# Attention units of a transformer block: the order of ScalarE's first exponentials, two groups of sums, the distance tables first, two more zero products

## The chip, the cores and the metric

The kernel runs on one core of one Trainium2 chip. The metric is the device time of one execution in microseconds (us). A core has five engines with instruction queues of their own: TensorE (PE), VectorE (DVE), ScalarE (ACT), GpSimd (POOL) and SyncE (SP), which here issues most DMA transfers. They meet through semaphores.

## The reference

Attention with a distance bias over q, k and v of 2 batches x 8 heads x 768 positions x 64, and behind it two feed-forward layers on the 1536 x 512 result:

```python
scores = scale * np.matmul(q, k.transpose(0, 1, 3, 2))
rel = pos[:, None] - pos[None, :]
is_global = pos[None, :] < int(n_global)                 # 8
is_local = (rel >= 0) & (rel < int(n_local))             # 96
keep = is_global | is_local
dist = np.where(is_global & ~is_local, float(n_local), np.abs(rel).astype(np.float32))
bias = -slopes[:, None, None] * dist[None, :, :]
scores = np.where(keep, scores + bias[None], -1000000000.0)
scores = scores - np.max(scores, axis=-1, keepdims=True)
a = np.exp(scores)
a = a / (np.sum(a, axis=-1, keepdims=True) + 1e-09)
x = np.matmul(a, v)                                      # then as 1536 x 512
...
h = x @ w_in;  g = h * (1.0 / (1.0 + np.exp(-h)));         x = g @ w_out      # 512 -> 2048 -> 512
h = x @ w_in;  g = h * np.clip(h + 3.0, 0.0, 6.0) / 6.0;   x = g @ w_out
```

## The kernel before

Attention is cut into 16 **units**: a batch, a half of the sequence (384 positions) and a pair of heads. A unit has three query tiles of 128 rows (HB = 3); because a row keeps only the 96 positions behind it and 8 global ones, each tile needs 128 columns of keys (the first of a first half) or 256. Units 0 to 3 are the first half of batch 0. The main loop runs in steps n = 3u + t, tile t of unit u, and does at each step a part of several units:

- `loads`, `loads_v`: SP issues the DMAs for keys rk, kp, queries rq and values rv, vp of units ahead (L230 to L251).
- `stage_a` (t = 0 keys, t = 1 queries of unit u + 1): PE transposes them into the bank psA (L329 to L338), ACT copies the keys to kt (L350) and scales the queries into qt (L331), DVE copies the global keys into kt (L351, and L353 in a second half).
- `scores` (t = 0): six products of PE into the banks psS (L369).
- `exponentials`: DVE adds the bias and takes the row minimum (L379: z, mn), then ACT takes the exponential with the sum beside it (L383: z, sm). Two heads make a pair of each.
- `normalise`, one unit later: DVE adds 1e-9 to the sums and takes the reciprocal (L388, L389), POOL multiplies z with it (L393).
- `turn` (t = 2 of the next unit): PE transposes z into psT (L403); the copies pt go to DVE (L408, tiles 0 and 2) and ACT (L406, tile 1).
- `values` (two units later): PE multiplies with v into psO (L421); ACT writes the rounded copy xh (L424), DVE the rest xl (L425).

The bias tables come first: `positions` (POOL, DVE), then `patterns` (DVE, L277 to L294), which needs the two words n_global and n_local (nwords, L741) and leaves distB and distA; `biases` (POOL, L314) scales them for each pair of heads into nbB and nbA. `beyond` (L300 to L305) writes a flag that tells whether n_global and n_local lie outside what the tiling covers; it is read long after. Three products of zeros (L739, into psW) open the work of PE.

Beside attention the first feed-forward weights are decoded into a high and a low part: ACT L103, L107, L145, DVE L986 to L1003, POOL L126, L134, L148 (wih and wil are the parts of the weight, raw, da, dc, de the steps to them). From step 17 on a feed-forward piece (`h_piece`, psH, L482, or `y_piece`, psY, L655) is put in at every second step, and behind the last unit only these are left.

PE, ACT and POOL execute in the order in which this code is written. DVE and SP are ordered by a scheduler during attention, from the written order and the dependencies. Buffers of z, pt and the psum banks go round, so a tile waits for the one that had its place before.

Of the kernel before, what the change touches and what calls it, by code (L numbers as in the profile page):

```python
# [18 lines left out]
P = 128  # L19
# [9 lines left out]
def attention_ffn_kernel(ctx, tc, q, k, v, n_global, n_local, w_in1, w_out1, w_in2, w_out2, out):  # L29
# [345 lines left out]
    def exponentials(u, t):  # L375
        p, w = units[u][2], width(u, t)
        nb, z, mn, sm = nbs[p][w == W], zt[u], mnt[u], smt[u]
        for h in range(2):
            nc.vector.tensor_tensor_reduce(  # L379
                out=z[:, t, h, :w], in0=scored[u][h, t][:, :w], in1=nb[:, h, :], scale=1.0, scalar=3e38,  # L380
                op0=ALU.add, op1=ALU.min, accum_out=mn[:, t, h:h + 1])
        for h in range(2):
            nc.scalar.activation(out=z[:, t, h, :w], in_=z[:, t, h, :w], func=AF.Exp, bias=mn[:, t, h:h + 1], scale=-1.0,  # L383
                                 accum_out=sm[:, t, h:h + 1])

    def normalise(u):
        z, sm = zt[u], smt[u].rearrange("p t h -> p (t h)")
        nc.vector.tensor_scalar(out=sm, in0=sm, scalar1=1e-9, scalar2=None, op0=ALU.add)  # L388
        nc.vector.reciprocal(sm, sm)  # L389
        for t in range(HB):  # L390
            w = width(u, t)
            for h in range(2):
                nc.gpsimd.tensor_scalar(out=z[:, t, h, :w], in0=z[:, t, h, :w], scalar1=smt[u][:, t, h:h + 1], scalar2=1.0,  # L393
                                        op0=ALU.mult, op1=ALU.mult)
# [16 lines left out]
    def values(u):  # L411
# [12 lines left out]
        nc.scalar.copy(hi, ps[:, :TB])  # L424
        return lambda: nc.vector.tensor_tensor(out=lo, in0=ps[:, :TB], in1=hi.bitcast(F32), op=ALU.subtract)  # L425

    NS = HB * len(units)
    queue, late, rests, now = {}, {}, {}, [0]

# [3 lines left out]
    def attention_loop(n):  # L433
        u, t = divmod(n, HB)
        for f in queue.pop(n, []):
            f()
        if t == 0 and u < len(units):
            scores(u)
        if t == 0 and 0 <= u - 2 < len(units):
            at(n + 1, values(u - 2))  # L440
            if u < len(units):
                loads_v(u)
        if u < len(units):
            exponentials(u, t)
            if t == HB - 1 and u + 1 < NP:
                biases(u + 1)
        if n == 0:
            beyond()
        if t == 0 and 0 <= u - 1 < len(units):
            normalise(u - 1)  # L450
        for f in rests.pop(n, []):
            f()
        if t < 2 and u + 1 < len(units):
            stage_a(u + 1, t)
            if t and u + 3 < len(units):
                loads(u + 3)
# [277 lines left out]
    with tc.manual_schedule(engines=None):  # L734
        nc.vector.memset(three, 3.0)
        warm = fpool.tile([P, 512], F32, name="warm", tag="a")
        nc.vector.memset(warm, 0.0)
        for _ in range(3):
            nc.tensor.matmul(bank("f", "psW"), warm[:, :P], warm, start=True, stop=True)  # L739
        for i, ap in enumerate((n_global, n_local)):  # L740
            nc.sync.dma_start(nwords[:, i, :], ap.bitcast(I32).partition_broadcast(P))  # L741
        loads(0)
        make_identity(nc, ident)
        positions()
        loads(1)
        load_weights()
        loads_v(0)
        load_weights()
        loads(2)
        loads_v(1)  # L750
        load_weights()
        stage_a(0, 0)
        stage_a(0, 1)
        patterns()
        biases(0)
    todo = {when(i): f for i, f in enumerate(stream)}

    def loop(n):
# [277 lines left out]
```

## Time and profile before

| | |
|---|---|
| median of 3 runs | 636.79 us (635.8 to 637.16) |
| profiled execution | 634.86 us, its span 632.8 us |
| granted TensorE clock, mean | 0.992 of full speed |
| PE busy | 606.6 us (96%), 3124 products |
| DVE, ACT, POOL busy | 464.5 (73%), 412.9 (65%), 160.4 us (25%) |
| DMA | 97.29 MB, mean 154 GB/s |

The profiled execution has a start and an end of 2.06 us outside its span. A row of a timeline gives the start from the span's beginning, the duration, the engine, the line, the output and the inputs; in the brackets stands how long the engine had been idle just before and what released it. A row of the windows gives a stretch, its length and the busy time of PE, the weight loads of PE, DVE, ACT and POOL in it (with the number of instructions), then the clock that PE was granted, the busy share of the DMA engines, and GB/s. A clock of 1.00 is 2.4 GHz and 0.5 is 1.2 GHz; a stretch in which both occur has a mean between.

### The profile page before, as it was taken

The numbers are of one execution on the slowest core, as the hardware profiler recorded it, in microseconds if no ns is written. First come the engines' busy times: TensorE is split into PE (matmuls) and PEld (weight loads), VectorE is DVE, ScalarE is ACT, GpSimd is POOL, SyncE is SP. The second block draws the span as 40 slices with busy tenths as digits, with TensorE's granted clock in tenths as the row PEclk, the third lists the DMA queues.
The fourth block names the chain that finished last, engine by engine and source line by source line (L and its number), as shares of the span: only waits on it lengthen the run. The fifth ranks groups of instructions, "written<-read, shape, count | busy, mean of one in ns | idle before, by whom it ended". The sixth has DMA issues, their size and how long they took to land.

```text
span 632.8 us, 9365 instructions
## 1 busy us (share of the span) xinstructions
PE 606.6 (96%) x3124; PEld 496.4 (78%) x3124; DVE 464.5 (73%) x1012; ACT 412.9 (65%) x863; POOL 160.4 (25%) x233
## 2 busy tenths in 40 slices
PE   6877999999999999999999999999999999999996
PEld 3656778898888788888888877887788888888885
DVE  5776777734588786767674779987979696969453
ACT  4785878755566676666666676765766666666760
POOL 2764867770111111111111110011111111111100
PEclk9998999999999999999999999999999999999998
DMA  7665556367767858686867791196577768776544
GB/s 173 154 157 124 128 142 147 87 195 141 157 129 158 186 135 183 151 186 151 186 152 154 161 207 67 67 266 151 136 174 163 176 162 177 160 183 151 100 109 162
DMA packets 81622, 97.29 MB, mean 154 GB/s; under 512 B 55456, under 2 KB 55456, under 8 KB 81312
## 3 DMA queue, kind: packets, MB, share of 16 engines
q0 software_dynamic: 12576, 45.09, 38.1%
q1 hardware_dynamic: 68992, 51.53, 27.2%
q8 instruction: 27, 0.44, 0.3%
q14 instruction: 27, 0.22, 0.1%
HBM read 46.27 MB, written 3.15 MB: 78 GB/s over the span
## 4 chain that ended last, share of the span: by engine, by line
PE 58%; issue 23%; POOL 6%; DVE 5%; ACT 5%; DMA 2%; POOLq 0%; DVEq 0%; SPq 0%; ACTq 0%
PE psY L655 25%; PE psH L482 15%; POOL y L684 4%; PE psP_b L563 3%; PE psO L421 3%; PE psT L403 2%; PE psP_c L563 2%; PE psP_a L563 2%; PE psS_S L369 2%; ACT z L383 2%; DMA y<-st 1%; POOL z L393 1%; PE psW L739 1%; PE psS_o L369 1%; DVE z L379 1%
## 5 line engine op out<-in xcount | busy, mean ns | idle before, releaser
L684 POOL DMA_DIRECT2D y<-st x78 | 66.9, 857 | 364.3 <-ACT st L680 359.1
L680 ACT COPY st<-psY 128x512 f32<-128x512 f32 x156 | 91.5, 587 | 52.0 <-PE psY L655 47.9
L482 PE MATMUL psH<-xh,wih 128*128 128x512 f32 (+1 forms) x216 | 83.3, 386 | 2.1 <-DVE g L513 1.5
L482 PE MATMUL psH<-xh,wil 128*128 128x512 f32 (+1 forms) x216 | 82.7, 383 | 2.3 <-POOL wil L148 2.3
L482 PE MATMUL psH<-xl,wih 128*128 128x512 f32 (+1 forms) x216 | 82.7, 383 | 0.0
L655 PE MATMUL psY<-gh,woh 128*128 128x512 f32 (+1 forms) x160 | 61.4, 384 | 0.0
L655 PE MATMUL psY<-gh,wol 128*128 128x512 f32 (+1 forms) x160 | 60.6, 379 | 0.0
L655 PE MATMUL psY<-gl,woh 128*128 128x512 f32 (+1 forms) x160 | 60.5, 378 | 0.0
L655 PE MATMUL psY<-woh,gl 128*128 128x512 f32 x144 | 56.1, 390 | 0.1
L655 PE MATMUL psY<-woh,gh 128*128 128x512 f32 x144 | 56.1, 390 | 0.1
L655 PE MATMUL psY<-wol,gh 128*128 128x512 f32 x144 | 56.0, 389 | 0.0
L393 POOL TENSOR_SCALAR z<-z,sm 128x256 f32<-128x256 f32 (+1 forms) x96 | 45.9, 501 | 26.8 <-DVE sm L389 20.3
L383 ACT ACTIVATE z<-z,mn 128x256 f32<-128x256 f32 (+1 forms) x96 | 46.4, 489 | 3.8 <-DVE mn L379 3.7
L482 PEld LDWEIGHTS psH<-xh,wih 128*128 128x128 f32 x216 | 40.6, 188 | 10.6 <-DVE g L513 1.9
L482 PEld LDWEIGHTS psH<-xh,wil 128*128 128x128 f32 x216 | 40.7, 188 | 9.8 <-POOL wil L148 2.7
L103 ACT ACTIVATE da<-raw 128x512 f32<-128x512 f32 x64 | 43.0, 672 | 6.7 <-DMA raw<-in_moe_w_in_dram 5.3
L482 PEld LDWEIGHTS psH<-xl,wih 128*128 128x128 f32 x216 | 40.7, 188 | 7.5 <-DVE xl L592 0.4
L998 DVE SCALAR_TENSOR_TENSOR da<-raw,da 128x512 int32<-128x512 int32 x64 | 44.2, 690 | 1.1
L986 DVE TENSOR_SCALAR da<-da 128x512 f32<-128x512 f32 x64 | 29.5, 461 | 15.9 <-ACT da L103 15.6
L580 DVE TENSOR_TENSOR u<-psP_c,u 128x512 f32<-128x512 f32 x22 | 15.1, 686 | 34.6 <-ACT u L574 34.6
L504 ACT ACTIVATE a<-psH 128x512 f32<-128x512 f32 (+1 forms) x24 | 14.2, 590 | 40.2 <-PE psH L482 40.2
L523 DVE SCALAR_TENSOR_TENSOR gl<-a,gh 128x512 fp32r<-128x512 f32 (+1 forms) x34 | 23.1, 681 | 22.4 <-ACT gh L517 22.1
(187 smaller groups left out, 1496.9 us busy)
## 6 DMA issues: line engine op xcount, KB each, us to landing
y<-st POOLq DMA_DIRECT2D x78, 512.0 KB, 5.0
raw<-in_moe_w_in_dram SPq DMA_DIRECT2D x32, 512.0 KB, 4.0
raw<-in_moe_w_out_dram SPq DMA_DIRECT2D x32, 512.0 KB, 3.6
rk<-in_k_dram SPq DMA_DIRECT2D x32, 96.0 KB, 3.4
rq<-in_q_dram SPq DMA_DIRECT2D x32, 96.0 KB, 2.5
rv<-in_v_dram SPq DMA_DIRECT2D x32, 96.0 KB, 2.4
out_dram<-y SPq DMA_DIRECT2D x12, 256.0 KB, 2.6
xf<-xh SPq DMA_DIRECT2D x2, 1024.0 KB, 5.2
```

Of the source, the lines that this page charges most:

```text
L103: nc.scalar.activation(out=t["a"], in_=raws[n][:, :, 1].bitcast(F32), func=AF.Abs)
L369: nc.tensor.matmul(place[h, t], qt[hs, t * P:(t + 1) * P], kt[hs, o:o + W], start=True, stop=True)
L383: nc.scalar.activation(out=z[:, t, h, :w], in_=z[:, t, h, :w], func=AF.Exp, bias=mn[:, t, h:h + 1], scale=-1.0, accum_out=sm[:, t, h:h + 1])
L393: nc.gpsimd.tensor_scalar(out=z[:, t, h, :w], in0=z[:, t, h, :w], scalar1=smt[u][:, t, h:h + 1], scalar2=1.0, op0=ALU.mult, op1=ALU.mult)
L482: nc.tensor.matmul(ps, a[:, kt, js], x[:, kt, n0:n1], start=n == 0, stop=n == 3 * KT - 1)
L523: nc.vector.scalar_tensor_tensor(out=gl[:, j, :], in0=t["a"], scalar=2.0, in1=gh[:, j, :].bitcast(F32), op0=ALU.mult, op1=ALU.subtract)
L563: nc.tensor.matmul(ps, a[:, 2 * k + q, f * P:(f + 1) * P], x, start=p in (1, 5) and n == 0, stop=n == 5, skip_group_check=True)
L655: nc.tensor.matmul(ps[:, :rhs.shape[1]], lhs, rhs, start=n == 0, stop=n == 3 * FC - 1)
L680: nc.scalar.copy(st[:, m % 2, :], part)
L684: late.setdefault(n, []).append(lambda: nc.gpsimd.dma_start(y, st, accum_op=ALU.add))
L986: nc.vector.tensor_scalar(out=a, in0=a, scalar1=as_float(897 << 20), scalar2=as_float((1151 << 20) - 1), op0=ALU.max, op1=ALU.min)
L998: nc.vector.scalar_tensor_tensor(out=ai, in0=w1, scalar=-0x40000000, in1=ai, op0=ALU.bitwise_and, op1=ALU.bitwise_or)
```

## The change

Five things are moved or added, all in the attention part.

1. `exponentials(u, 0)` is now written ahead of `values(u - 2)`, so that ACT takes the first pair of exponentials of a unit ahead of the copy xh.
2. `normalise` is split: the sums of tiles 0 and 1 are taken at step t = 1 of the unit itself, those of tile 2 at t = 2. Before, all six came at t = 0 of the next unit.
3. `patterns` and `biases(0)` are written ahead of unit 0's `stage_a`; `biases` of the next unit move from t = 2 to t = 0.
4. `beyond` moves from step 0 to step 30.
5. Two more products of zeros stand at step 2, ahead of unit 1's scores on PE.

```diff
--- before.py
+++ after.py
@@ -383,11 +383,11 @@
             nc.scalar.activation(out=z[:, t, h, :w], in_=z[:, t, h, :w], func=AF.Exp, bias=mn[:, t, h:h + 1], scale=-1.0,
                                  accum_out=sm[:, t, h:h + 1])
 
-    def normalise(u):
-        z, sm = zt[u], smt[u].rearrange("p t h -> p (t h)")
+    def normalise(u, t0, t1):
+        z, sm = zt[u], smt[u][:, t0:t1].rearrange("p t h -> p (t h)")
         nc.vector.tensor_scalar(out=sm, in0=sm, scalar1=1e-9, scalar2=None, op0=ALU.add)
         nc.vector.reciprocal(sm, sm)
-        for t in range(HB):
+        for t in range(t0, t1):
             w = width(u, t)
             for h in range(2):
                 nc.gpsimd.tensor_scalar(out=z[:, t, h, :w], in0=z[:, t, h, :w], scalar1=smt[u][:, t, h:h + 1], scalar2=1.0,
@@ -424,6 +424,11 @@
         nc.scalar.copy(hi, ps[:, :TB])
         return lambda: nc.vector.tensor_tensor(out=lo, in0=ps[:, :TB], in1=hi.bitcast(F32), op=ALU.subtract)
 
+    def warm_up(n):
+
+        for _ in range(n):
+            nc.tensor.matmul(bank("f", "psW"), warm[:, :P], warm, start=True, stop=True)
+
     NS = HB * len(units)
     queue, late, rests, now = {}, {}, {}, [0]
 
@@ -434,22 +439,24 @@
         u, t = divmod(n, HB)
         for f in queue.pop(n, []):
             f()
-        if t == 0 and u < len(units):
-            scores(u)
+        if u < len(units):
+            if t == 0:
+                scores(u)
+                if u + 1 < NP:
+                    biases(u + 1)
+            exponentials(u, t)
+            if t:
+                normalise(u, *((0, 2), (2, 3))[t - 1])
         if t == 0 and 0 <= u - 2 < len(units):
             at(n + 1, values(u - 2))
             if u < len(units):
                 loads_v(u)
-        if u < len(units):
-            exponentials(u, t)
-            if t == HB - 1 and u + 1 < NP:
-                biases(u + 1)
-        if n == 0:
+        if n == 30:
             beyond()
-        if t == 0 and 0 <= u - 1 < len(units):
-            normalise(u - 1)
         for f in rests.pop(n, []):
             f()
+        if n == 2:
+            warm_up(2)
         if t < 2 and u + 1 < len(units):
             stage_a(u + 1, t)
             if t and u + 3 < len(units):
@@ -735,8 +742,7 @@
         nc.vector.memset(three, 3.0)
         warm = fpool.tile([P, 512], F32, name="warm", tag="a")
         nc.vector.memset(warm, 0.0)
-        for _ in range(3):
-            nc.tensor.matmul(bank("f", "psW"), warm[:, :P], warm, start=True, stop=True)
+        warm_up(3)
         for i, ap in enumerate((n_global, n_local)):
             nc.sync.dma_start(nwords[:, i, :], ap.bitcast(I32).partition_broadcast(P))
         loads(0)
@@ -749,10 +755,10 @@
         loads(2)
         loads_v(1)
         load_weights()
+        patterns()
+        biases(0)
         stage_a(0, 0)
         stage_a(0, 1)
-        patterns()
-        biases(0)
     todo = {when(i): f for i, f in enumerate(stream)}
 
     def loop(n):
```

What this makes of the engines' queues is shown at three places. In the names the first digit is the unit and the last number a buffer: kt3 are the keys of unit 3.

DVE at the start of the program, two pieces of the difference (+ is after, - before; distA and pat2 are the tables, small and nval the words, psA0_0 the transposed keys, psS0 the scores of unit 0):

```order
 L271 CAST pat2_87<-pat1_86 128x128
 L272 TENSOR_SCALAR pat2_87<-distA_83 128x256
-L351 COPY kt0_157<-psA0_0_159 128x2x32
 L277 SCALAR_TENSOR_TENSOR small_85<-nwords_82 128x2
 L278 SCALAR_TENSOR_TENSOR nval_59<-small_85,nwords_82 128x2
```

```order
 L294 TENSOR_SCALAR distA_83<-distA_83,nval_59 128x32
 L284 TENSOR_SCALAR pat2_87<-pat2_87 128x256
-L379 ISA z0_203,mn0_204<-psS0_S0_193,nbB0_184 128x128
+L285 TENSOR_TENSOR distA_83<-distA_83,pat2_87 128x256
+L351 COPY kt0_176<-psA0_0_178 128x2x32
+L379 ISA z0_203,mn0_204<-psS0_S0_193,nbB0_170 128x128
 L379 ISA mn0_204 128x1
```

The copy of unit 0's keys has moved from ahead of the tables to behind the last of them, and the first reduction stands behind both.

ACT between units 1 and 2, before and after:

```order
L406 COPY pt0_1_335<-psT0_1_330 128x512
L424 CAST xh_80<-psO0_358 128x384
L383 ACTIVATE z2_355,sm2_357<-z2_355,mn2_356 128x128 x2
L350 COPY kt3_390<-psA3_0_392 128x3x128
L103 ACTIVATE da1_400<-raw1_137 128x512
```

```order
L406 COPY pt0_1_345<-psT0_1_340 128x512
L383 ACTIVATE z2_365,sm2_367<-z2_365,mn2_366 128x128 x2
L424 CAST xh_80<-psO0_378 128x384
L350 COPY kt3_398<-psA3_0_400 128x3x128
L103 ACTIVATE da1_408<-raw1_137 128x512
```

The pair of exponentials of unit 2 and the copy xh of unit 0's values have changed places; so it is in each later unit.

DVE at the end of unit 2, before and after:

```order
L425 TENSOR_TENSOR xl_81<-psO0_358,xh_80 128x384
L408 COPY pt1_0_437<-psT1_0_434 128x2x128
L351 COPY kt3_390<-psA3_0_392 128x2x32
L986 TENSOR_SCALAR da1_400<-da1_400 128x512
L992 TENSOR_SCALAR da1_400<-da1_400 128x512
L998 SCALAR_TENSOR_TENSOR da1_400<-raw1_137,da1_400 128x512
L1003 TENSOR_SCALAR de1_535<-da1_400 128x512
L408 COPY pt1_2_451<-psT1_2_446 128x512
L379 ISA z3_467,mn3_468<-psS3_S0_457,nbB3_428 128x128
```

```order
L425 TENSOR_TENSOR xl_81<-psO0_378,xh_80 128x384
L351 COPY kt3_398<-psA3_0_400 128x2x32
L992 TENSOR_SCALAR da1_408<-da1_408 128x512
L408 COPY pt1_0_449<-psT1_0_446 128x2x128
L998 TENSOR_SCALAR da1_408<-da1_408 128x512
L388 TENSOR_SCALAR sm2_367<-sm2_367 128x4
L1004 SCALAR_TENSOR_TENSOR da1_408<-raw1_137,da1_408 128x512
L389 RECIPROCAL sm2_367<-sm2_367 128x4
L1009 TENSOR_SCALAR de1_545<-da1_408 128x512
L408 COPY pt1_2_463<-psT1_2_458 128x512
L388 TENSOR_SCALAR sm2_367<-sm2_367 128x2
L379 ISA z3_479,mn3_480<-psS3_S0_469,nbB3_368 128x128
```

The sums of unit 2 (sm2) now stand in unit 2 itself, the second group just ahead of the first reduction of unit 3; the copy of unit 3's keys has come ahead of the copy pt1_0. (Line numbers behind the change are 6 higher in the last part of the file.)

## Rows read from the trace of the kernel before

**Rows 1.** Windows by engine of units 2 to 4, unit 5, units 6 to 15, the rest

```profile
20.42:41.22 20.80, 15.89 (x148) 11.84 (x148) 16.94 (x61) 15.47 (x53) 17.23 (x30) 1.00 0.64 145
41.22:52.91 11.69, 9.25 (x63) 7.78 (x63) 6.36 (x25) 7.76 (x24) 5.51 (x9) 0.85 0.66 162
52.91:126.00 73.09, 68.68 (x602) 56.38 (x602) 55.49 (x206) 57.26 (x184) 50.81 (x78) 1.00 0.52 125
126.00:632.80 506.80, 498.46 (x2254) 412.71 (x2252) 374.35 (x664) 322.15 (x576) 79.95 (x94) 1.00 0.68 157
```

**Rows 2.** Timeline of PE: start, duration, engine, line, tiles, count, [idle before <- releaser]

```profile
1.50 5.08 PE L739 MATMUL psW<-warm 128*128 128x512 f32 x6 [1.50 <-DVE warm L737]
...
8.14 1.13 PE L369 MATMUL psS_S<-kt,qt 64*128 64x256 f32 x8 [0.58 <-DVE nval L278]
...
14.64 1.58 PE L369 MATMUL psS_S<-kt,qt 64*128 64x256 f32 x8 [3.81 <-ACT qt L331]
...
20.42 1.13 PE L369 MATMUL psS_S<-kt,qt 64*128 64x256 f32 x8
...
49.07 0.50 PE L482 MATMUL psH<-xh,wil 128*128 128x384 f32 x1 [2.34 <-POOL wil L148]
```

**Rows 3.** Windows around two stretches of PE at a lower granted clock

```profile
14.60:18.70 4.10, 4.06 (x20) 2.80 (x21) 3.11 (x16) 2.98 (x11) 1.25 (x4) 0.58 0.52 106
49.10:52.90 3.80, 3.80 (x16) 3.49 (x16) 0.96 (x3) 1.06 (x2) 1.43 (x2) 0.55 0.63 142
```

**Rows 4.** Timeline of all engines, at the start

```profile
1.21 0.42 SPq L741 DMA_DIRECT2D nwords<-in_n_local_dram  x1
...
7.77 0.15 DVE L277 SCALAR_TENSOR_TENSOR small<-nwords 128x2 f32<-128x2 int32 x1
...
10.80 0.27 DVE L379 CUSTOM_DVE_ANT_0 z<-psS_S,nbB 128x128 f32<-128x128 f32 x1
...
11.01 0.56 DVE L285 TENSOR_TENSOR distA<-distA,pat 128x256 f32<-128x256 f32 x1
```

**Rows 5.** DMA issues: tile, queue, count, KB each, us from issue to landing

```profile
rq<-in_q_dram SPq DMA_DIRECT2D x32, 96.0 KB, 2.5
...
nwords<-in_n_local_dram SPq DMA_DIRECT2D x1, 1.0 KB, 3.3
```

**Rows 6.** Timeline of ACT in units 1, 2 and 4

```profile
16.58 0.40 ACT L383 ACTIVATE z<-z,mn 128x128 f32<-128x128 f32 x1 [0.45 <-DVE mn L379]
...
18.25 0.48 ACT L350 COPY kt<-psA 128x384 f32<-128x384 f32 x1 [0.54 <-PE psA L338]
...
23.28 0.48 ACT L424 CAST xh<-psO 128x384 fp32r<-128x384 f32 x1 [1.74 <-PE psO L421]
...
37.41 0.48 ACT L424 CAST xh<-psO 128x384 fp32r<-128x384 f32 x1 [2.22 <-PE psO L421]
...
38.78 0.46 ACT L350 COPY kt<-psA 128x384 f32<-128x384 f32 x1
```

**Rows 7.** Timeline of POOL in units 0, 4 and 5

```profile
17.45 2.55 POOL L393 TENSOR_SCALAR z<-z,sm 128x128 f32<-128x128 f32 x6 [4.02 <-DVE sm L389]
...
45.03 2.76 POOL L393 TENSOR_SCALAR z<-z,sm 128x256 f32<-128x256 f32 x6 [3.93 <-PE psA L336]
47.75 1.27 POOL L148 TENSOR_TENSOR wil<-dc,wih 128x512 fp32r<-128x512 f32 x1
```

**Rows 8.** Line 388, VectorE's addition to the sums: shortest, median, longest in ns

```profile
L388 DVE TENSOR_SCALAR sm<-sm x16: 160/170/1206, 16.5 to 128.3; 128x6 f32<-128x6 f32 x16
```

**Rows 9.** Timeline of all engines at the start of unit 2

```profile
21.70 0.29 DVE L379 CUSTOM_DVE_ANT_0 z<-psS_S,nbB 128x128 f32<-128x128 f32 x1 [0.47 <-PE psS_S L369]
...
21.82 1.27 POOL L126 TENSOR_TENSOR dc<-dc,de 128x512 f32<-128x512 f32 x1
...
21.91 1.21 DVE L388 TENSOR_SCALAR sm<-sm 128x6 f32<-128x6 f32 x1
```

**Rows 10.** Timeline of SP: unit 3's two loads of queries

```profile
19.26 0.91 SPq L237 DMA_DIRECT2D rq<-in_q_dram  x2
```

## Prediction

> **What bounds the kernel now.** I read the page first: TensorE (PE) is busy for 96% of the span, so only its idle time and its stretches at a lower clock can be won. Then windows by stage say where these lie [rows 1]. From 126 us to the end only feed-forward work is left, and PE is busy for 498.46 of 506.80 us there: it is a conveyor, and whatever is gained ahead of 126 us arrives at the end one for one. Units 2 to 4 of attention leave PE idle for 20.80 − 15.89 = 4.91 us, unit 5 for 11.69 − 9.25 = 2.44, units 6 to 15 for 73.09 − 68.68 = 4.41. Unit 5 also runs at a mean granted clock of 0.85. PE's own timeline shows the start [rows 2]: scores of unit 0 at 8.14, of unit 1 at 14.64 behind 3.81 us of idle time, of unit 2 at 20.42, and at 49.07 a first feed-forward product that waited 2.34 us for POOL. Windows around two stretches show the clock: 14.60 to 18.70 at 0.58 and 49.10 to 52.90 at 0.55, about 1.2 instead of 2.4 GHz, each behind one of these idle gaps [rows 3]. Last come the timelines of the other engines, to see what these gaps waited for.
>
> **The start.** VectorE (DVE) begins the distance tables (L277) at 7.77 and ends them (L285) at 11.01 + 0.56 = 11.57, so 3.80 us, in which one of unit 0's reductions (10.80 to 11.01) has its place [rows 4]. The tables need the two words of nwords, issued from 1.21 [rows 4] and landing 3.3 us later [rows 5], at about 4.5. In before, L277 stands behind the copy of unit 0's keys (L351), which waits for a load and for PE. The change puts that copy behind the tables. They then run from 4.5 to about 4.5 + 3.80 − 0.21 = 8.1. The copy has no row of its own here; it costs between nothing and the 0.56 of the far larger L285 [rows 4], and I take 0.4 for it and its hand-over: scores of unit 0 at 8.6 instead of 8.14, a loss of 0.46. But the first reduction no longer waits for tables and biases. In unit 2 it stands 21.70 − 20.42 = 1.28 behind the scores [rows 2, 9], which makes 9.9 here instead of 10.80 [rows 4]: **0.9 us earlier** on DVE and ScalarE (ACT), whose first exponentials and copy of the queries release unit 1's scores. So these start at about 13.7. Below, nothing is gained if a load, not the tables, decides; above, all of the 10.80 − 8.6 = 2.2 less a minimum of 0.27 for the reduction itself, so 1.9.
>
> **Two more zero products** stand on PE between unit 1's transposes of queries and its scores. Six records of the first three took 5.08 us [rows 2], 1.7 a product; two make 3.4, which fits into the 3.81 of idle time (2.9 if the start is 0.9 earlier; 0.5 at worst sticks out). At full clock they are shorter; by the 1.13 against 1.58 us of the same eight scores of units 0 and 1 [rows 2] they would take 2.4. I cost them at nothing, covered by the wait for the queries. What they bring: the gap ahead of unit 1 is filled, so the 4.10 us at 0.58 [rows 3] should run at about 1.00. In that stretch ACT waited 0.45 for a reduction and 0.54 for PE's transposes [rows 6], so a full clock gives 0.99, and unit 1 lasts 5.78 − 0.99 = 4.8 instead of 20.42 − 14.64 = 5.78. Together the scores of unit 2 start at 13.7 + 4.8 = 18.5: **gain 1.9**, from 0 (the clock does not hold, a load decides) to 1.9 + 4.06 × (1 − 0.58) = 3.6.
>
> **Units 2 to 4: ACT's order.** In before ACT takes the copy xh of the values of unit u − 2 (L424) ahead of the first two exponentials of unit u, and stands 1.74 us waiting for PE in unit 2 and 2.22 in unit 4 [rows 6], with the reductions long ready in part of it: unit 2's first is at 21.70 [rows 9], ACT's wait ends at 23.28. The pair then costs 2 × 0.40 in a narrow unit such as 2 or 3 and 38.78 − 37.41 − 0.48 = 0.89 in unit 4, ahead of the copy of the next keys (L350), on which everything of the next unit stands. The change moves the pair into the wait: 0.8 + 0.8 + 0.9, **gain 2.5**. Below it is 0, if something else (loads) sets these units; above it is PE's whole idle time, 4.91 [rows 1]. What it costs: xh comes later if the pair is not ready when PE is; 1.74 against 0.8 leaves room.
>
> **Sums in two groups.** DVE's addition and reciprocal on the sums now come twice, 128x4 and 128x2: 32 more small instructions, 0.17 us each by the median [rows 8], 0.34 a unit. DVE is idle for 20.80 − 16.94 = 3.86 us in units 2 to 4 [rows 1], so I cost them at nothing. POOL's scaling can start one step sooner and ends sooner. In unit 0 it waited 4.02 us for the sums, in unit 4 3.93, where the names in the bracket are only what came last [rows 7]. That counts in **unit 5**: POOL scaled z(4) from 45.03 to 47.79 and only then made wil (1.27 us) [rows 7], for which PE waited 2.34 us [rows 2], and fell to the lower clock, losing 3.80 × (1 − 0.55) = 1.71 more [rows 3]. With the scaling 2 to 4 us earlier, wil is ready before PE asks. PE's idle 2.44 and the 1.71 go: 4.15. Against it stands a new wait: the third sum waits for ACT's last pair, and behind it on DVE are the next unit's reductions, or the copy pt of unit 5. I take 0.5 for it, a little over one exponential of 0.40 [rows 6]: **gain 3.7**, bounds 2.3 (only POOL's wait) and 4.15.
>
> **Units 6 to 15.** The same two moves act on PE's 4.41 us idle; I take half, **2.2**, with 0.5 and 4 as bounds, since no row says which part is ACT's order and which the loads or the weight decoding.
>
> **The rest** costs nothing: the range flag (L300 to L305) keeps its place on DVE and only its reading moves; the biases run on POOL, which is idle there. SP's order of loads changes little.
>
> A row speaks against the smaller groups. One of the 16 additions took 1206 ns instead of 170 [rows 8]: at 21.91, while POOL ran L126 from 21.82 for 1.27 [rows 9]. It seems held by POOL. The Trainium skill ("GPSIMD Engine Reference", section "1. Specifications") says that GpSimd's SBUF interfaces are shared with VectorE, with contention for DVE instructions in a two-port mode or with two SBUF inputs. By that rule any of the new additions that meets a POOL instruction may be held so, and the sum would be smaller by about a microsecond for each on the path; by the rows it was one of 16, and off by 1.04.
>
> **Sum.** 1.9 + 2.5 + 3.7 + 2.2 = 10.3. The profiled execution lasted 634.86 us (span 632.8), so 624.6 by it; the median of the runs, 636.79, lies 1.93 above, and I keep that: **626.5 us**.
>
> **Rivals.**
> *Loads decide.* SP issues unit 3's loads of queries at 19.26, taking 0.91 for two [rows 10]; they land 2.5 later [rows 5], at about 22.7, and 12 or more such issues a unit at 0.46 are 5.5 us of a unit of about 7. If units 2 to 4 can't come closer than SP feeds them, their 2.5 goes, and half of the 2.2 of units 6 to 15: 626.5 + 3.6 = **630.1**. For it: SP is close to full. Against it: PE's waits in the rows are on ACT and POOL.
> *All idle time goes.* Between 20.42 and 126 PE has 4.91 + 4.15 + 4.41 = 13.5 to give, of which I take 8.4; with all of it 626.5 − 5.1 = **621.4**.
> *Sums held by POOL: slower.* All 16 new additions meet POOL's work, as the one of [rows 8] did, with DVE's reductions queued behind each: 16 × 1.04 = 16.6, less 10.3, is +6.3: **643.1**. It decides from 10 held additions on (10 × 1.04 = 10.4). For it: POOL is busy for 17.23 of 20.80 us there [rows 1], and the second group stands ahead of the next unit's reductions. Against it: of the additions so far one was hit, though POOL was as busy.
> *It reaches the path only at the start.* Unit by unit something else is late by as much, and only 1.9 is left: **634.9**.
>
> **How the numbers follow.** The forecast has 0.57, loads 0.19, all idle time 0.09, held sums 0.07, start alone 0.08. The range 621.0 to 631.0 takes in the first three and drops the last two and a little of each tail, so about 0.8. A measurement of this kernel tells about 0.2% (1.3 us) from no change: faster is 0.57 + 0.19 + 0.09 and 0.03 of the last, 0.88; within 0.2% the other 0.05 of the last; slower 0.07.
>
> **What would show it.** Scores of unit 1 near 13.7 and of unit 2 near 18.5, with the granted clock near 1.00 between; if they stand at 14.6 and 20.4, the first two steps are wrong. Units 2 to 4 shorter by 2.5 in sum, with ACT's wait ahead of xh filled by exponentials; unchanged, with PE or ACT waiting on DMA, it is the loads. No wait for wil and no low clock near 47 us. L388 x32 with a median of 0.17; many near 1.2 are the held sums. From the first feed-forward stretch on, the same 507 us. A start that is lost to a load, or PE waiting in unit 5 for something else, would break the forecast most.

## The result, and the profile after

The changed kernel takes **625.88 us** (median of 4 runs, 625.52 to 626.57) against 636.29 for the kernel before (median of 4, 634.59 to 637.16): a ratio of 0.9841, 95% interval 0.9817 to 0.9864, or 10.4 us less. The forecast was 626.5. Its profiled execution took 625.65 us with a span of 623.5; by the two profiled executions the gain is 634.86 − 625.65 = 9.2 us.

First the windows by stage of the kernel after (from : to, length, busy time of PE, PEld, DVE, ACT and POOL, granted clock, DMA share, GB/s), which answer to [rows 1]: units 2 to 4, unit 5, units 6 to 14, unit 15 with the last of attention, the rest.

```profile
18.37:37.61 19.24, 16.31 (x149) 11.85 (x148) 16.37 (x66) 16.17 (x53) 15.88 (x29) 1.00 0.71 170
37.61:45.26 7.65, 7.57 (x64) 6.28 (x64) 6.33 (x28) 7.32 (x24) 5.62 (x11) 1.00 0.80 190
45.26:109.61 64.35, 61.74 (x551) 51.28 (x550) 54.35 (x206) 54.22 (x168) 42.41 (x67) 1.00 0.62 147
109.61:124.89 15.28, 14.51 (x137) 12.38 (x137) 11.09 (x30) 9.89 (x31) 14.19 (x19) 1.00 0.45 141
124.89:623.50 498.61, 489.98 (x2169) 405.45 (x2169) 370.46 (x655) 317.22 (x562) 72.30 (x84) 1.00 0.68 156
```

The same three last stages of the kernel before, cut at the same instructions. (The cut at 126 us in [rows 1] was too early: the last products of attention stand at 134 us.)

```profile
52.91:119.80 66.89, 62.48 (x551) 51.37 (x550) 50.09 (x186) 51.81 (x167) 45.60 (x71) 1.00 0.54 131
119.80:134.50 14.70, 14.68 (x137) 12.26 (x137) 9.36 (x28) 10.20 (x32) 11.69 (x17) 1.00 0.44 141
134.50:632.80 498.30, 489.98 (x2169) 405.46 (x2169) 370.39 (x655) 317.40 (x562) 73.47 (x85) 1.00 0.68 157
```

The feed-forward part is the same to 0.3 us with the same 2169 products: what attention gains arrives at the end. Unit 5 shows the largest part of it: 7.65 us for 11.69, and a clock of 1.00 for 0.85.

PE's own timeline after (start, duration, engine, line, tiles, [idle before <- releaser]), against [rows 2]:

```profile
8.74 1.13 PE L369 MATMUL psS_S<-kt,qt 64*128 64x256 f32 x8 [0.58 <-ACT qt L331]
...
11.27 2.21 PE L430 MATMUL psW<-warm 128*128 128x512 f32 x4
...
13.75 1.13 PE L369 MATMUL psS_S<-kt,qt 64*128 64x256 f32 x8 [0.27 <-ACT qt L331]
...
18.37 1.13 PE L369 MATMUL psS_S<-kt,qt 64*128 64x256 f32 x8
...
21.64 0.52 PE L329 MATMUL psA<-ident,rk 128*128 128x128 f32 x3 [0.46 <-DMA rk<-in_k_dram]
...
22.57 0.52 PE L329 MATMUL psA<-ident,rq 128*128 128x128 f32 x3 [0.24 <-DMA rq<-in_q_dram]
...
30.14 1.65 PE L403 MATMUL psT<-ident,z 128*128 128x128 f32 x10 [0.92 <-DVE xl L425]
...
35.83 1.65 PE L403 MATMUL psT<-ident,z 128*128 128x128 f32 x10 [0.39 <-DVE xl L425]
```

Scores of unit 1 stand at 13.75 and of unit 2 at 18.37; the wait for wil is gone. New are small waits for the loads rk and rq in unit 2. The waits for xl in units 3 and 4 are not new; the kernel before had them at the same places (PE before):

```profile
32.54 0.41 PE L403 MATMUL psT<-ident,z 128*128 128x128 f32 x2 [0.92 <-DVE xl L425]
...
38.73 0.41 PE L403 MATMUL psT<-ident,z 128*128 128x128 f32 x2 [0.46 <-DVE xl L425]
```

The length of each stage, from one start of the scores to the next in one profiled execution of each kernel, is the measure of the experiments. "Tail" runs from unit 15's scores to the last group of products with the values. Medians are of all runs of a kernel; the kernel before had medians of 636.0 to 636.5 beside them. One execution's stages and the median of several can differ by a microsecond or two.

| kernel | unit 0 | unit 1 | 2 to 4 | unit 5 | 6 to 14 | tail | median us |
|---|---|---|---|---|---|---|---|
| before | 6.50 | 5.78 | 20.80 | 11.69 | 66.89 | 14.26 | 636.29 |
| after | 5.01 | 4.62 | 19.24 | 7.65 | 64.35 | 14.84 | 625.88 |
| no_zeros | 4.97 | 4.62 | 21.44 | 7.65 | 64.36 | 14.83 | 625.71 |
| copy_first | 6.51 | 4.62 | 18.72 | 7.66 | 64.39 | 14.87 | 626.29 |
| no_start | 6.50 | 6.27 | 18.77 | 7.69 | 64.37 | 14.85 | 627.53 |
| xh_first | 4.98 | 4.62 | 22.25 | 7.43 | 66.64 | 14.77 | 629.94 |
| six_sums | 6.23 | 5.46 | 18.67 | 10.21 | 63.89 | 14.16 | 629.52 |
| one_group | 4.99 | 5.28 | 19.07 | 10.30 | 64.05 | 14.99 | 628.12 |
| late_biases | 4.98 | 8.09 | 22.70 | 7.42 | 64.38 | 14.65 | 632.06 |
| b_groups | 6.36 | 7.29 | 22.66 | 7.42 | 66.65 | 14.61 | 637.03 |
| b_groups_biases | 6.51 | 6.29 | 20.03 | 7.43 | 66.63 | 14.77 | 631.20 |
| b_exp | 6.52 | 5.60 | 19.32 | 10.20 | 63.90 | 14.18 | 629.68 |
| loads_ahead | 5.01 | 4.62 | 18.72 | 7.64 | 64.40 | 14.82 | 626.23 |
| own_bank | 5.01 | 4.62 | 17.76 | 7.89 | 65.52 | 14.85 | 624.84 |

### The profile page after: what moved, and what is told of

Read it like the earlier page. It is cut to its first block, busy times and chain, and to the rows that moved or that the text cites. A ratio compares the mean times of both kernels' runs of the same rounds, so it can differ in the third digit from the quotient of the medians.

```text
span 623.5 us, 9408 instructions
## 1 busy us (share of the span) xinstructions
PE 605.3 (97%) x3128; PEld 494.9 (79%) x3128; DVE 470.6 (75%) x1044; ACT 414.7 (67%) x863; POOL 158.0 (25%) x233
## 4 chain that ended last, share of the span: by engine, by line
PE 36%; issue 25%; POOL 5%; DVE 2%; DMA 2%; ACT 1%; POOLq 0%; ACTq 0%; SPq 0%; DVEq 0%
PE psY L662 20%; PE psH L489 9%; POOL y L691 5%; PE psP_b L570 3%; PE psP_c L570 2%; PE psP_a L570 2%; DMA y<-st 1%; DMA raw<-in_moe_w_in_dram 1%; ACT st L687 0%; DVE g L520 0%; DVE da L1004 0%; DVE wol L148 0%; DVE u L587 0%; DVE dc L134 0%; ACT da L103 0%
## 5 line engine op out<-in xcount | busy, mean ns | idle before, releaser
L393 POOL TENSOR_SCALAR z<-z,sm 128x256 f32<-128x256 f32 (+1 forms) x96 | 43.5, 471 | 32.3 <-DVE sm L389 25.0
L489 PEld LDWEIGHTS psH<-xh,wih 128*128 128x128 f32 x216 | 40.6, 188 | 10.4 <-DVE g L520 2.2
L1004 DVE SCALAR_TENSOR_TENSOR da<-raw,da 128x512 int32<-128x512 int32 x64 | 46.0, 718 | 1.0
```

What stands on the lines that cost most here:

```text
L489: nc.tensor.matmul(ps, a[:, kt, js], x[:, kt, n0:n1], start=n == 0, stop=n == 3 * KT - 1)
L1004: nc.vector.scalar_tensor_tensor(out=ai, in0=w1, scalar=-0x40000000, in1=ai, op0=ALU.bitwise_and, op1=ALU.bitwise_or)
```

## The experiments

### The start: no_zeros, copy_first, no_start

The kernel after without the two more products of zeros:

```diff
-        if n == 2:
-            warm_up(2)
```

> The changed kernel without its two more zero products. Theory (the products hold the clock): scores of unit 1 still at about 13.75 us, but behind an idle gap of PE of about 2.5 us, then a stretch near 0.58 of the clock; unit 1 lasts 5.6 instead of 4.62, scores of unit 2 near 19.4, time 626.9. Rival (the gap is now short enough, or unit 2 waits for its loads anyway): unit 2's scores within 0.3 of 18.37, time 625.9.

Measured: 625.71 us. Unit 1 lasts 4.62 all the same, and PE's clock held although PE was idle for 2.28 us ahead of unit 1's scores (13.49). The rival holds: the products bring nothing here that a measurement could tell. (In the profiled execution, the longest of the four with 626.83, unit 2 was long: DVE was held there, as told in the last section.)

The kernel after with the tables behind unit 0's transposes again:

```diff
-        patterns()
-        biases(0)
         stage_a(0, 0)
         stage_a(0, 1)
+        patterns()
+        biases(0)
```

> The changed kernel with the distance tables written behind unit 0's transposes again. Theory (the tables decide the first reduction): scores of unit 0 at 8.1, first reduction near 10.8, scores of unit 1 near 14.6 instead of 13.75, time 626.8. Rival (a load of unit 1 or 2 decides by now): scores of unit 2 within 0.3 of 18.37 and 625.9 us.

Measured: 626.29 us. Unit 0 takes the 6.5 us of before, so the tables do decide its length: 1.5 us. Unit 1 keeps 4.62, behind an idle gap of 1.77. What of the 1.5 is left at the end is uncertain: 0.4 by the medians, less than a measurement tells apart, and 1.1 by the stages. Units 2 to 4 last 18.72 instead of 19.24, since unit 2 no longer comes ahead of its loads.

Both taken out, that is both diffs above at once:

> The changed kernel with both edits of the start taken out: tables behind unit 0's transposes, no two more zero products. Each of them alone cost nothing to leave out (625.71 without the products, 626.29 with the tables late). Theory (they cover for each other: either holds the clock in unit 1, tables by a shorter gap, products by filling it): now the gap ahead of unit 1's scores is 3.8 us, unit 1 runs near 0.58 of the clock and lasts 5.5 to 5.8 instead of 4.62, scores of unit 2 near 20.4 or later, 627.3 to 628.5. Rival (the start is worth nothing at all, since unit 2 waits for its loads): 625.5 to 626.5 with unit 3's scores near 26.4 in either case.

Measured: 627.53 us, and unit 1 lasts 6.27. The granted clock of unit 1 in the four kernels tells why (windows over unit 1, columns as above): no_start, then copy_first, no_zeros and the kernel after.

```profile
15.26:21.53 6.27, 6.17 (x30) 4.31 (x30) 4.31 (x21) 4.66 (x17) 4.07 (x11) 0.62 0.83 203
```

```profile
15.68:20.30 4.62, 3.92 (x29) 2.90 (x29) 4.00 (x21) 4.27 (x16) 3.49 (x9) 1.00 0.80 212
```

```profile
13.49:18.11 4.62, 3.99 (x30) 2.90 (x30) 3.71 (x22) 4.27 (x16) 3.41 (x9) 1.00 0.68 146
```

```profile
13.70:18.30 4.60, 3.91 (x29) 2.90 (x29) 3.74 (x22) 4.25 (x16) 3.34 (x9) 1.00 0.73 148
```

The same products (one record is missing in two of the windows) take 6.17 us at 0.62 behind a gap of 3.80, and about 3.95 in the three others. The two edits of the start cover for each other: in these executions one of them is enough for the clock, and together they are worth 627.53 − 625.88 = 1.65 us by the medians, 2.7 by the stages.

### ACT's order: xh_first, b_exp

The kernel after with the values, and so xh, written ahead of the first exponentials again:

```diff
                 scores(u)
                 if u + 1 < NP:
                     biases(u + 1)
+                if u >= 2:
+                    at(n + 1, values(u - 2))
             exponentials(u, t)
 ...
         if t == 0 and 0 <= u - 2 < len(units):
-            at(n + 1, values(u - 2))
             if u < len(units):
                 loads_v(u)
+            else:
+                at(n + 1, values(u - 2))
```

> The changed kernel with ACT's copy xh ahead of the first exponentials again. Theory (the order of ACT bought 1.56 us in units 2 to 4 and some of the 2.5 in units 6 to 14): units 2 to 4 last 20.4 to 20.8 instead of 19.24 us, time 627.5 to 629. Rival (in units 3 and 4 of the changed kernel PE waits 0.92 and 0.39 us for xl, so the later xh gives back what the exponentials win): 625.5 to 626.3.

Measured: 629.94 us, 4.1 more, above the theory's range. Units 6 to 14 go back to 66.64, and units 3 and 4 together from 12.54 to 13.76. Units 2 to 4 took 22.25, more than the theory's 20.8, because unit 2 took 8.49 in this execution, with 1.45 of PE's idle time put down to rq. SP issued that load at 19.03, and at 19.06 in the kernel after, so I do not count this part as ACT's order.

The other way round, the kernel before with nothing but ACT's order of the change:

```diff
+            if u < len(units):
+                exponentials(u, t)
             at(n + 1, values(u - 2))
             if u < len(units):
                 loads_v(u)
         if u < len(units):
-            exponentials(u, t)
+            if t or u < 2:
+                exponentials(u, t)
```

> The kernel before with nothing but the first pair of exponentials ahead of xh. Theory (this order alone gives about 1.2 us in units 3 and 4 and 2.3 in units 6 to 14): units 6 to 14 last 64.4 to 64.8 instead of 66.89, unit 5 still waits for wil, time 632 to 633.5. Rival (with the sums one unit late the exponentials are no gain): units 6 to 14 above 66, time above 635.

Measured: 629.68 us, 6.3 less than 636.01 beside it, and 2.3 below the theory's range. Units 6 to 14 give 2.99 (the theory had 2.1 to 2.5) and units 2 to 4 1.48. The surprise is unit 5: PE still waits 2.38 us for wil, but its clock stays up, and the unit lasts 10.20 instead of 11.69.

```profile
47.83 0.44 PE L485 MATMUL psH<-xh,wil 128*128 128x384 f32 x1 [2.38 <-POOL wil L148]
```

```profile
47.83:50.04 2.21, 2.21 (x16) 2.00 (x16) 0.77 (x3) 0.76 (x2) 1.19 (x1) 1.00 0.68 153
```

These are PE's row and the window behind it in b_exp. Compare [rows 2, 3]: the same wait in the kernel before, 2.34, was followed by 0.55. So 1.5 us of unit 5's loss went away in a kernel that has only ACT's order of the change. Why the clock held is not shown, and each side rests on few executions (this one and six_sums against the one of before).

### The sums: six_sums, one_group

The kernel after with all six sums one unit later, as before:

```diff
             exponentials(u, t)
-            if t:
-                normalise(u, *((0, 2), (2, 3))[t - 1])
 ...
+        if t == 0 and 0 <= u - 1 < len(units):
+            normalise(u - 1, 0, HB)
```

> The changed kernel with the sums of a unit taken together, one unit later, as before. Theory (the earlier sums free POOL for wil): PE waits some 2 us for wil in unit 5 and falls to about 0.55 of the clock, unit 5 lasts 11 to 11.7 instead of 7.65, time 629.5 to 631. Rival (the start and the order of ACT bring wil in time): unit 5 stays below 8.5, time 626 to 626.8.

Measured: 629.52 us, 3.6 more; unit 5 lasts 10.21. PE waits 2.38 us for wil as the theory said, but the clock stays at 1.00 there, as in b_exp. POOL's rows show the cause: the scaling of z(4) and the product wil, first in six_sums, then in the kernel after.

```profile
44.47 2.75 POOL L393 TENSOR_SCALAR z<-z,sm 128x256 f32<-128x256 f32 x6 [3.91 <-DVE sm L389]
47.19 1.26 POOL L148 TENSOR_TENSOR wil<-dc,wih 128x512 fp32r<-128x512 f32 x1
```

```profile
38.92 2.81 POOL L393 TENSOR_SCALAR z<-z,sm 128x256 f32<-128x256 f32 x6 [1.73 <-DVE sm L389]
41.70 1.29 POOL L148 TENSOR_TENSOR wil<-dc,wih 128x512 fp32r<-128x512 f32 x1
```

Unit 5 begins at 40.50 in six_sums and at 37.61 after; POOL begins 3.97 us into it in the one and 1.31 in the other: 2.66 us earlier, about what PE waited and what unit 5 lost (2.56).

The rest of the 3.6 is not accounted for. Of the other stages, units 2 to 4, units 6 to 14 and the tail are 1.7 shorter together in six_sums, and unit 1 is 0.8 longer. Unit 0 began 1.4 later and took 1.2 longer in this execution, with products at half their pace before any sum is taken, which the edit can't have done; the theory's 629.5 to 631 was reached, but not by the low clock that it had in its sum.

Are two groups needed, or is it enough to be early? The six sums together at the unit's own last step:

```diff
-            if t:
-                normalise(u, *((0, 2), (2, 3))[t - 1])
+            if t == HB - 1:
+                normalise(u, 0, HB)
```

> The changed kernel with all six sums of a unit taken together at its own last step: early, but in one group. Theory (being earlier is what counts, the groups do not): unit 5 stays below 8.2, time 625.5 to 626.5. Rival (POOL needs the first four sums early to be through with the scaling): wil comes about 1.3 us later, POOL's scaling of unit 4 starts near 40.2 instead of 38.9, PE waits about 1 us for it in unit 5; time 627 to 629.

Measured: 628.12 us, and unit 5 takes 10.30. The theory falls. POOL got its sums at 41.88 only (unit 5 began at 37.84), and PE waited for wil (rows of one_group, POOL and PE):

```profile
41.88 2.77 POOL L393 TENSOR_SCALAR z<-z,sm 128x256 f32<-128x256 f32 x6 [2.76 <-DVE sm L389]
```

```profile
45.93 0.44 PE L489 MATMUL psH<-xh,wil 128*128 128x384 f32 x1 [1.72 <-POOL wil L148]
```

What the common addition (L388) lost is its place on DVE. ACT's last pair of unit 4, which it needs, was through at 39.34, but it ran at 41.11 only, behind two steps of the weight decoding and a copy pt. In the kernel after the first group of four sums runs at 37.85, ahead of them. Chance is in it too: two decoding steps took 1.15 and 1.38 us on DVE instead of their median of 0.42, while POOL had a product running (here the second, POOL and DVE):

```profile
37.78 1.33 POOL L134 TENSOR_TENSOR dc<-dc,da 128x512 f32<-128x512 f32 x1
```

```profile
38.02 1.38 DVE L998 TENSOR_SCALAR da<-da 128x512 int32<-128x512 int32 x1
```

Counted from the start of unit 5 the addition is 3.0 us later than the first group in the kernel after, and these two holds are 1.7 of it; what one group costs without them was not measured.

### What the groups need: b_groups, late_biases, b_groups_biases

The kernel before with nothing but the sums in two groups:

```diff
             exponentials(u, t)
+            if t:
+                normalise(u, *((0, 2), (2, 3))[t - 1])
             if t == HB - 1 and u + 1 < NP:
                 biases(u + 1)
 ...
-        if t == 0 and 0 <= u - 1 < len(units):
-            normalise(u - 1)
```

> The kernel before with nothing but the sums in two groups. Theory (this edit alone takes the wait for wil and the low clock out of unit 5): unit 5 below 8.5 instead of 11.69, units 2 to 4 as before within 0.6, time 632 to 633 against 636. Rival (ACT's late exponentials of before keep the sums late, so POOL gets no earlier start): unit 5 above 10, time above 634.5.

Measured: 637.03 us, a ratio of 1.0015 (0.9998 to 1.0032): no gain at all. Yet unit 5 lasts 7.42 instead of 11.69. Units 1 to 3 lost 3.4 of the 4.3 us that it won: 23.29 for 19.91. In unit 1 the first reduction of b_groups (DVE) shows the wait:

```profile
18.23 0.29 DVE L379 CUSTOM_DVE_ANT_0 z<-psS_S,nbB 128x128 f32<-128x128 f32 x1 [1.74 <-POOL nbB L314]
```

POOL executes in the order of the code. The earlier scaling now stood ahead of the next unit's biases nbB and nbA, which the code of before writes at t = 2, behind it. The change also moves the biases to t = 0, a line that the prediction took for free. So the kernel after with that one line moved back:

```diff
                 scores(u)
-                if u + 1 < NP:
-                    biases(u + 1)
             exponentials(u, t)
             if t:
                 normalise(u, *((0, 2), (2, 3))[t - 1])
+            if t == HB - 1 and u + 1 < NP:
+                biases(u + 1)
```

> The changed kernel with the biases of the next unit written at step t = 2 again, behind the scaling of z on POOL. The kernel before with the two groups alone gained 4.3 us in unit 5 and lost 3.4 in units 1 to 3, where the first reduction waited 1.74 and 1.90 us for nbB. Theory (with the sums early, POOL's scaling now stands ahead of the next unit's biases; moving the biases ahead is what makes the early sums pay): units 1 to 3 last 2.5 to 4 us longer in sum than in the changed kernel (17.97), time 628.5 to 630. Rival (the biases cost nothing, as the prediction had it, and the loss came of something else in the kernel before): 625.5 to 626.3.

Measured: 632.06 us, 6.2 more, which is more than the theory had, and the largest part of any edit taken out of the kernel after. Units 1 to 3 last 8.09, 7.95 and 8.13: 24.17 for 17.97, as much as the medians differ. The rows of unit 1 in late_biases: POOL, then DVE, then PE; and DVE's first reduction in the kernel after.

```profile
14.45 2.55 POOL L393 TENSOR_SCALAR z<-z,sm 128x128 f32<-128x128 f32 x6 [5.36 <-DVE sm L389]
16.96 0.69 POOL L314 TENSOR_SCALAR nbB<-distB 128x128 f32<-128x128 f32 x2
```

```profile
17.30 0.29 DVE L379 CUSTOM_DVE_ANT_0 z<-psS_S,nbB 128x128 f32<-128x128 f32 x1 [1.90 <-PE psT L403]
```

```profile
19.71 1.94 PE L403 MATMUL psT<-ident,z 128*128 128x128 f32 x8 [2.33 <-DVE kt L351]
```

```profile
14.91 0.29 DVE L379 CUSTOM_DVE_ANT_0 z<-psS_S,nbB 128x128 f32<-128x128 f32 x1 [0.38 <-PE psS_S L369]
```

POOL scales for 2.55 us, then makes nbB from 16.96, two in 0.69, so the first is there at about 17.3; the reduction that reads nbB starts at 17.30 instead of 14.91. The bracket names psT, which merely came last by the records: in this row the biases are seen by their time alone. PE then waits 2.33, and its products of 1.13 behind it take 2.08: the low clock makes the loss larger than the wait.

And the kernel before with the groups and the biases together:

```diff
+            if t == 0 and u + 1 < NP:
+                biases(u + 1)
             exponentials(u, t)
-            if t == HB - 1 and u + 1 < NP:
-                biases(u + 1)
+            if t:
+                normalise(u, *((0, 2), (2, 3))[t - 1])
```

> The kernel before with the sums in two groups and the biases moved ahead of the scaling, nothing else. Theory: unit 5 again near 7.4, units 1 to 3 within 0.7 of the 19.9 us of before instead of 23.3, time 631.5 to 633.5. Rival (the sums are no gain without ACT's order): above 634.5.

Measured: 631.20 us, 4.8 less than 636.01: unit 5 stays at 7.43, and units 1 to 3 last 19.66. The groups are worth their 4.3 us only with the biases out of the way. The biases were not moved alone.

### What is left: loads_ahead, own_bank

The kernel after with unit 3's loads issued ahead of unit 1's values and the third weight load:

```diff
         loads(2)
-        loads_v(1)
-        load_weights()
 ...
                 loads(u + 3)
+                if u == 0:
+                    loads_v(1)
+                    load_weights()
```

> The changed kernel with unit 3's loads of keys and queries issued ahead of unit 1's values and of the third weight load, 4 us earlier on SP. Theory (in the changed kernel unit 2 is set by these loads: PE waited 0.46 and 0.24 us, ACT 0.66 for what follows): unit 2 lasts 5.9 to 6.2 instead of 6.70, no wait of PE for rk or rq there, time 624.8 to 625.4. Rival (the values or the weight, now 3 us later, are late instead, or something else in unit 2 takes the time): 625.6 to 626.5.

Measured: 626.23 us (625.24 to 628.52). Unit 2 lasts 6.06 instead of 6.70 and PE's waits for rk and rq are gone, as the theory said; but the total is not less. In its profiled execution unit 0 began 0.7 later and the feed-forward part took 1.7 longer, neither of which lies where the loads were moved; such differences between executions are larger than the 0.6.

In addition the values of units 0 to 2 in the idle bank of the feed-forward products:

```diff
-        ps = bank("tr", f"psO{u}")
+        ps = bank("f" if u < 3 else "tr", f"psO{u}")
```

> The changed kernel with unit 3's loads ahead of unit 1's values, and with the values of units 0 to 2 (psO) in the bank of the feed-forward products, which is idle then, so that the transposes psT of z need not wait until xl has read the bank they shared. Theory (PE's waits of 0.92 and 0.39 us in units 3 and 4 of the changed kernel are this hand-over of a bank): units 2 to 4 last 17.4 to 18.2 us instead of 19.24, no wait for xl there, time 624 to 625.3. Rival (something else is as late, ACT's copy pt or the scaled z): 18.5 or more, 625.5 to 626.5.

Measured: 624.84 us median of 6, four of them between 624.25 and 624.89, two at 627.42 and 627.93. Units 2 to 4 last 17.76, 1.48 less than after, and PE no longer waits for xl there: the theory holds for these units. It is the lowest median here, but 1.0 us below the changed kernel is less than the 1.3 that a measurement tells apart. One of the two long runs is the profiled one, and shows what came instead. In unit 7 PE waits for queries; SP's two issues took 2.06 us, against 0.90 for the same two after (rows of own_bank, PE and SP; then SP after):

```profile
55.90 0.52 PE L329 MATMUL psA<-ident,rq 128*128 128x128 f32 x3 [0.89 <-DMA rq<-in_q_dram]
```

```profile
51.56 2.06 SPq L237 DMA_DIRECT2D rq<-in_q_dram  x2
```

```profile
49.44 0.90 SPq L237 DMA_DIRECT2D rq<-in_q_dram  x2
```

In this execution a load sets unit 7. The range flag's move was not tried alone; its instructions stand between the same steps of the tables on DVE, before and after.

## Why the prediction was right, and where it was not

The time and the sign came out: 626.5 forecast, 625.88 measured; 10.3 forecast, 9.2 by the profiled executions and 10.4 by the medians. That it is so close is partly luck. The profiled executions gained 1.1 us less than the sum, and the median, which lay 1.93 above the profile and was expected to stay there, lies only 0.23 above it after: an error of 1.1 and one of 1.7, of opposite sign. Step by step, by the profiles:

**The start: right in time, wrong in its reason for the second part.** The words landed and the tables began at 4.64 (4.5 forecast), the first reduction stood at 10.02 (9.9), scores at 13.75 and 18.37 (13.7 and 18.5): 2.05 us for 1.9. DVE's rows after:

```profile
4.64 0.16 DVE L277 SCALAR_TENSOR_TENSOR small<-nwords 128x2 f32<-128x2 int32 x1 [2.27 <-DMA nwords<-in_n_local_dram]
...
10.02 0.29 DVE L379 CUSTOM_DVE_ANT_0 z<-psS_S,nbB 128x128 f32<-128x128 f32 x1 [1.57 <-POOL nbA L314]
```

The bracket names POOL's nbA, so the biases may still hold the first reduction a little: it stands 1.28 behind its scores, and 1.16 in unit 1.

But the step put the restored clock down to the zero products. In no_zeros the tables first kept it up by themselves; that two edits could buy the same thing was not asked. And not all of the 2.05 reaches the end, since unit 2 then waits for its loads, some 0.5 us: with both edits taken out the time grows by 1.65.

**Units 2 to 4: the mechanism right, the size off.** 1.56 for 2.5. ACT's rows after show that the pair moved into the wait, and what ACT waits for next:

```profile
19.98 0.40 ACT L383 ACTIVATE z<-z,mn 128x128 f32<-128x128 f32 x1 [0.21 <-DVE mn L379]
...
21.23 0.48 ACT L424 CAST xh<-psO 128x384 fp32r<-128x384 f32 x1 [0.36 <-PE psO L421]
...
22.36 0.48 ACT L350 COPY kt<-psA 128x384 f32<-128x384 f32 x1 [0.66 <-PE psA L338]
...
27.91 0.40 ACT L383 ACTIVATE z<-z,mn 128x128 f32<-128x128 f32 x1 [0.61 <-DVE mn L379]
...
28.70 0.46 ACT L424 CAST xh<-psO 128x384 fp32r<-128x384 f32 x1
```

In unit 2 the wait ahead of xh fell from 1.74 [rows 6] to 0.36, but ACT then waits 0.66 for keys that PE can't transpose yet, as rk has not landed: 0.27 of the expected 0.8. In unit 3 the pair itself waits 0.61 for its minimum, and PE waits 0.92 for the bank that xl reads, as long as before. DVE's rows after show why ACT's order could not shorten that: xh is through at 29.16, but xl stands behind unit 3's reductions on DVE.

```profile
29.10 0.42 DVE L379 CUSTOM_DVE_ANT_0 z<-psS_o,nbA 128x256 f32<-128x256 f32 x1
...
29.44 0.55 DVE L425 TENSOR_TENSOR xl<-psO,xh 128x384 fp32r<-128x384 f32 x1
```

DVE has no idle time from 24.28 to there, and the first step in that stretch is the held one of the last section. loads_ahead took the wait for the loads out, and own_bank the one for xl as well; the units became 0.52 and, with both, 1.48 shorter. The term took the whole pair as gained and did not ask which other waits of the unit the pair does not touch: PE's for xl, which stood in the profile before, and DVE's queue.

**Unit 5: right, 4.04 for 3.7.** Two things were not seen: the low clock there was gone with ACT's order alone (b_exp), and the price of 0.5 for the third sum did not come (PE is busy for 7.57 of 7.65).

**Units 6 to 15: 1.65 for 2.2.** Units 6 to 14 gave 2.54, from ACT's order (xh_first gives 2.29 of it back). The tail took 0.58 and the rest 0.31; with the sums late the tail is 14.16 (six_sums), so the early groups cost the tail about 0.6. The traces show where. PE waits 0.64 for DVE's reductions of unit 15, and two decoding steps among these took 1.07 and 0.83 us instead of 0.42 while POOL's products ran beside them (PE, DVE and POOL after):

```profile
114.55 0.45 PE L662 MATMUL psY<-gh,woh 128*128 128x384 f32 x1 [0.64 <-DVE mn L379]
```

```profile
111.64 1.07 DVE L992 TENSOR_SCALAR da<-da 128x512 f32<-128x512 f32 x1
```

```profile
111.42 1.01 POOL L533 TENSOR_TENSOR gl<-g,gh 128x384 fp32r<-128x384 f32 x1
```

In six_sums POOL does these products at other times, the two steps take 0.42 each, and PE does not wait there; in b_groups, with the groups, they take 0.81 and 0.83 and PE waits 0.73. No run was made to test it.

**"The rest costs nothing": a wrong reason.** The biases were taken as free because POOL "is idle there". Its own row [rows 1] has POOL busy for 17.23 of 20.80 us. The sum was not hurt only because the change makes both moves; 6.2 us hang on that line (late_biases).

**The rivals.** Loads decide in unit 2 alone, for some 0.5 us. No sum was held as in [rows 8], though other instructions of DVE were, as above and in the last section; the longest of the 32 (rows of line 388 after) took 651 ns:

```profile
L388 DVE TENSOR_SCALAR sm<-sm x32: 154/170/651, 13.9 to 118.5; 128x4 f32<-128x4 f32 x16, 128x2 f32<-128x2 f32 x16
```

The edits don't add up: alone, ACT's order gives 6.3 and the groups with their biases 4.8, the start in the kernel after 1.65, together 12.8 for 10.4. Of the surplus 1.7 is unit 5, where b_exp gains 1.49 and b_groups_biases 4.26 but both edits only 4.04: its lost clock is counted twice. The rest is less than a measurement tells apart.

## What to carry to other kernels

Ask of every instruction that is moved earlier on an engine that works in program order what it now stands ahead of: here an early scaling was worth nothing until the biases that it overtook were moved too. A gap that lets the clock fall can have two remedies, and then each looks free to leave out; take both away before either is called worthless. Where a wait is filled with other work, list the other waits of the same stage first: one that the move does not touch (here PE's for xl and a shared bank, and then the loads) stays, and only what lies above it is gained. Work that is moved on one engine also meets other work beside it: here POOL's products held DVE, which no step of the sum had priced.

## What the hardware showed that was not expected

An idle gap's length alone does not tell whether PE's clock falls. Behind 2.34 us in the kernel before it fell to 0.55 [rows 2, 3]; behind 2.38 in b_exp and six_sums, at the same place in the program, it stayed at 1.00. Both happen within one execution, too: in no_zeros it stayed at 1.00 behind 2.28 and fell to 0.50 behind 2.18, where four transposes take 1.09 us instead of 0.63 (PE in no_zeros).

```profile
13.49 1.13 PE L369 MATMUL psS_S<-kt,qt 64*128 64x256 f32 x8 [2.28 <-ACT qt L331]
...
25.86 1.09 PE L403 MATMUL psT<-ident,z 128*128 128x128 f32 x4 [2.18 <-DVE pt L408]
```

In late_biases it fell to 0.57 behind 1.95.

The three products of zeros that open every kernel took 5.01 us in one profiled execution (xh_first) and 6.34 in another (six_sums), and unit 0 began at 8.5 and 10.1: the start alone spreads the runs by over a microsecond. In six_sums the clock reads 1.00 from 10.14 us on, while its first eight scores took 2.08 instead of 1.13; there the column and the durations don't agree, and the durations are what the time follows.

DVE was held by POOL, though not in the sums. Two rows of the kernel after:

```profile
24.26 1.27 POOL L134 TENSOR_TENSOR dc<-dc,da 128x512 f32<-128x512 f32 x1
24.28 1.53 DVE L998 TENSOR_SCALAR da<-da 128x512 int32<-128x512 int32 x1
```

The 64 instructions of that line have a median of 0.42 us; this one took 1.53 while POOL's ran. In no_zeros one of the step before it (also 0.42 by the median) took 2.12, with PE waiting 2.18 behind it. The ends tell how long the hold lasts: DVE's step ends 0.28 us behind POOL's product here, 0.29 in no_zeros, and 0.28 and 0.29 in one_group. The Trainium skill ("GPSIMD Engine Reference", section "1. Specifications") names a contention of the two engines for DVE instructions in a two-port mode or with two SBUF inputs. The rows agree that there is one, and no run here shows which mode an instruction was in.
